# w_in's transform folded over d: two products a pair of chunks in place of four, E's coefficients through DRAM, and the third rounding step on VectorE and GpSimd

## The chip, the cores and the metric

One NeuronCore of one Trainium2 chip runs the whole kernel. The metric is device time in microseconds of one execution. The program has five engines that each run their own instructions in order and wait for one another through semaphores: TensorE (PE, with its weight loads as PEld), VectorE (DVE), ScalarE (ACT), GpSimd (POOL) and SyncE (SP), which here only issues DMAs.

## What is computed

A Fourier mixing layer and then a feed-forward layer with a squared ReLU:

```python
X = np.fft.fft(x, axis=1)                 # x: (8, 3008, 256) f32
X = np.fft.fft(X, axis=2).real            # real part only, f32
h = X.reshape(24064, 256) @ w_in          # w_in: (256, 2048)
g = np.maximum(h, 0.0) ** 2
out = g @ w_out                           # w_out: (2048, 256), out (24064, 256) f32
```

w_in and w_out arrive in double precision and are rounded to single precision inside the kernel.

## The kernel before

The second Fourier transform, over d = 256, is not done on x. Since it is linear, it is put into w_in: the kernel makes G1 (cosines over d, times w_in) and G2 (sines), each [128, 2048], and later multiplies them with Pt and Qt, the transform of x over the sequence. What is left over is column d = 128 of the frequencies, E; its part enters as a coefficient gE (one number for each of the 2048 features) times a row of E (`ew`). So one block of h is G1ᵀPt + gE·E ± G2ᵀQt.

**Pairs.** w_in and w_out come in eight pairs of 256 features each. A pair of w_in goes through four rounding steps, each a function that `convert` returns, and each a token in a written order: TS on DVE (the sign bits, L299), PW on ACT (three instructions, L306 to L308: scale the exponent, take the upper mantissa bits, and the third rounding step, a Relu into integers), H on DVE (L314, sign and exponent together), PR on GpSimd (L323, an integer addition that puts sign, exponent and mantissa together). Pairs of w_out go through the same four steps; their names have a w (TSw0 and so on). Pair 0 and 1 are rounded before the written order begins.

Then `dft_win` (L341 to L346) multiplies a rounded pair with a table over d: for cosines (`pgC`) and for sines (`pgD`) two products each, over the two halves of d, 256 columns wide. Each such product is two matmul records in the trace. `keep_win` (GC, GD; L350) copies the sums to G1 or G2 on ACT. `ends_of` (fe, L356) takes G2's last row, which holds the alternating sum, across to the partitions with two one-column products, and `keep_ends` (gE, L360) halves the result on DVE into gE.

**Order.** The string ORDER lists tokens for the first ten blocks; every token issues its instructions on its engines at that place, so the string fixes each engine's order. Besides the tokens above: f3a and f3b are the two halves of h's block 3 on TensorE (`front_half`, L986 and L988, two products of 252 columns), d3a and d3b their sums on DVE (`split_half`, L1001, L1003, L1004; the first reads gE), rl and sq the Relu and square on ACT, bk the eight records of the second layer (`plain`, L1107), sc and su the sums of w_out's parts (ACT L383, DVE L390). ph has two PSUM banks, so f waits for the d two halves earlier. H frees a raw buffer and lets SP load another pair (L285, two DMAs of 256 KB). After ORDER a regular loop runs over the blocks of eight batches, six column blocks of eight pairs each.

**Before ORDER.** The first batch of x is folded: over the sequence (`fold`: f_s, f_d; L541, L546), over d (f_sc, f_dc; L550, L554, with 129 and 128 columns left) and into even and odd frequencies (f_w, L559). f_e (L562, ACT) writes the folded column 128 into the last column of `lone`, from which the products E0 to E6 run. Each tile's products P, Q follow. Later batches are folded in pieces beside the products (`fold_later`: rows_of, columns_of, parities_of).

**Tables.** `cosd` and `sind` hold cosines and sines for d in two halves of 128, loaded by two DMAs.

Of the kernel before, what the change touches and what calls it, by code (L numbers as in the profile page):

```python
# [84 lines left out]
def kernel(  # L85
# [106 lines left out]
    cosd = const.tile([P, 2, P], F32, name="cosd")  # L192
    sind = const.tile([P, 2, P], F32, name="sind")
# [9 lines left out]
    G1 = const.tile([P, F], F32, name="G1")  # L203
    G2 = const.tile([P, F], F32, name="G2")
# [16 lines left out]
    def turn_table(t):  # L221
# [3 lines left out]
        for kp in range(2):  # L225
            nk = NC[kp][c]
            nc.scalar.mul(part_of(sinT, t)[0:rows, kp, at:at + nk], part_of(cosT, t)[0:rows, kp, at:at + nk][:, ::-1],
                          sind[0:rows, 0, P - 1:])
# [14 lines left out]
    for c in range(2):  # L243
        nc.vector.tensor_scalar(out=sind[:, c, P - 1:], in0=evens, scalar1=2.0, scalar2=-1.0,
                                op0=ALU.mult, op1=ALU.add)
# [43 lines left out]
    def convert(raw, dst, k):  # L289
# [12 lines left out]
        def powers():  # L302
# [5 lines left out]
            act(m.bitcast(U32), m, AF.Relu, bias=ramp[:, 1:2], scale=1.0)  # L308

        def halves():  # L310
            if high is None:
# [3 lines left out]
                                           op0=ALU.logical_shift_left, op1=ALU.bitwise_or)  # L315

        def product():
            to = dst()
            if high is None:
                nc.vector.tensor_copy(to, parts(low, k))  # L320
                return
            m, e = parts(st["m"], k), parts(st["e"], k)
            nc.gpsimd.tensor_tensor(out=to.bitcast(I32), in0=e.bitcast(I32), in1=m.bitcast(I32), op=ALU.add)  # L323
# [5 lines left out]
    def round_win(j, raw):  # L329
# [5 lines left out]
        return convert(raw, dst, 1)  # L335

    def round_wout(j, raw):
        return convert(raw, lambda: wout[:, j].rearrange("p h c e -> p h (c e)"), 2)

    def dft_win(j, side):  # L340

        tab, nm = ((cosd, "mC"), (sind, "mD"))[side]
        pg = psm.tile([P, CH], F32, name="pg", tag=nm) if j else psh.tile([P, CH], F32, name="pg", tag="h")
        for i in range(2):
            nc.tensor.matmul(pg, tab[:, i], win[j][:, i], start=i == 0, stop=i == 1)  # L345
        return pg  # L346

    def keep_win(j, side, pg):
        to, v = (G1, G2)[side].rearrange("p (h j f) -> j p h f", h=2, j=NJ)[j], pg.rearrange("p (h f) -> p h f", h=2)
        nc.scalar.copy(to, v)  # L350

    def ends_of(j):
        ps = psd.tile([P, CH], F32, name="pe", tag="d")
        for h in range(2):
            fc = j + NJ * h
            nc.tensor.matmul(ps[:, h:h + 1], G2[:, fc * P:(fc + 1) * P], last, start=True, stop=True)  # L356
        return ps
# [1278 lines left out]
```

## Time and profile before

| what | value |
|---|---|
| three timed runs, us | 1871.90, 1870.68, 1871.24; median 1871.24 |
| the profiled execution, its own time | 1871.07 us |
| its span, first to last instruction | 1869.3 us |
| granted TensorE clock over the span | 0.998 |
| rounding on GpSimd, L323 | 8 of w_in, 1294 ns (median); 8 of w_out, 1505 ns |
| DVE rounding steps | L299, 420 ns; L314, 684 ns, longest 1760 |
| ACT rounding steps | L306, 676 ns; L307, 756 ns; L308, 722 ns |
| products with the d tables, L345 | 64 records, 379 ns each, first at 15.5 us, last at 77.4 |
| edge products, L356 | 32 records, 250 ns each |
| copies to G1 and G2, L350 | 16, 372 ns |

A row of the timeline gives the start in us, the duration in us, engine, line, operation, what it writes and reads with its shape, how often, and in brackets how long the engine stood idle before it and who ended that. The duration of one record is not its cost on a full engine, because records overlap in the pipeline: the distance between the starts of two records that follow each other without a gap is the cost. Times below are us from the span's start.

### The profile page before, as it was taken

The page shows a single profiled execution, that of the slowest core. Times are in us where ns is not written, and L with a number is a line of the kernel's source. Part 1 is how long each engine was busy: PE and PEld are TensorE (multiplying, and loading weights), DVE is VectorE, ACT ScalarE, POOL GpSimd, SP SyncE. Part 2 cuts the span into 40 slices and gives each one's busy share as a digit, 9 for nine tenths or more (in the row PEclk, how much of TensorE's full clock was granted, in tenths as well). Part 3 has the DMA queues.
Part 4 walks back from the last instruction along what each step waited for, and adds up shares of the span by engine and source line. Part 5 has one row for each costly group of instructions (what it writes and reads, how often), then busy time and mean ns, then how long its engine had stood idle before and what let it go on. Part 6 is the DMA issues. An engine that isn't in the chain of part 4 may idle for free.

```text
span 1869.3 us, 34067 instructions
## 1 busy us (share of the span) xinstructions
PE 1854.7 (99%) x11408; PEld 1755.2 (94%) x11408; DVE 1466.6 (78%) x3480; ACT 1082.9 (58%) x1604; POOL 1465.4 (78%) x2149
## 2 busy tenths in 40 slices
PE   9999999999999999999999999999999999999998
PEld 7689999999999999999999999999999999999998
DVE  8788887887788877888788887888878887767665
ACT  5876645666466655556556565566645666444543
POOL 4489778888787887888878887788877878787886
PEclk9999999999999999999999999999999999999999
DMA  7441002100011111111011100111001100000000
GB/s 198 119 60 42 15 21 57 40 23 23 19 50 40 29 23 32 32 46 32 15 32 46 45 19 15 45 46 35 15 20 45 35 15 21 19 18 15 20 21 22
DMA packets 151309, 68.45 MB, mean 37 GB/s; under 512 B 131143, under 2 KB 142881, under 8 KB 151136
## 3 DMA queue, kind: packets, MB, share of 16 engines
q1 hardware_dynamic: 150590, 65.74, 14.0%
q8 instruction: 91, 1.49, 0.3%
q14 instruction: 82, 0.67, 0.1%
q0 software_dynamic: 416, 0.43, 0.1%
q10 hardware_dynamic: 130, 0.12, 0.0%
HBM read 41.54 MB, written 24.69 MB: 35 GB/s over the span
## 4 chain that ended last, share of the span: by engine, by line
PE 95%; DVE 3%; ACT 1%; issue 0%; POOL 0%; DMA 0%; DVEq 0%; POOLq 0%; ACTq 0%
PE F L1078 33%; PE S L1078 23%; PE hP L1015 17%; PE hQ L1015 17%; PE pd L745 2%; PE pd L868 1%; PE pd L842 1%; PE pg L345 0%; DVE wsum L390 0%; PE mA L1107 0%; PE mB L1107 0%; DVE he L1001 0%; DVE he L1019 0%; DVE g L1003 0%; PE ph L986 0%
## 5 line engine op out<-in xcount | busy, mean ns | idle before, releaser
L1028 ACT ACTIVATE g<-g 128x1008 f32<-128x1008 f32 (+1 forms) x384 | 399.4, 1040 | 304.6 <-DVE g L1024 285.3
L1019 DVE SCALAR_TENSOR_TENSOR he<-ew,gE,hP 128x252 f32<-128x252 f32 (+1 forms) x748 | 321.2, 471 | 290.2 <-PE hP L1015 290.2
L1031 ACT ACTIVATE g<-g 128x1008 f32<-128x1008 f32 (+1 forms) x384 | 399.4, 1040 | 12.1
L1015 PE MATMUL hP<-Pt,G 128*128 128x252 f32 (+1 forms) x1496 | 378.9, 376 | 3.3 <-DVE w L670 1.4
L1015 PE MATMUL hQ<-Qt,G 128*128 128x252 f32 (+3 forms) x1496 | 379.0, 376 | 0.3 <-DVE g L1024 0.3
L1078 PE MATMUL F<-s,wsum 128*128 128x168 f32 (+1 forms) x1504 | 337.1, 306 | 0.0
L1015 PEld LDWEIGHTS hQ<-Qt,G 128*128 128x128 f32 (+1 forms) x1496 | 281.9, 190 | 37.5 <-issue 2.4
L1078 PE MATMUL F<-g,wout 128*128 128x168 f32 (+1 forms) x1504 | 305.6, 305 | 0.0
L1053 POOL TENSOR_TENSOR s<-g 128x168 f32<-128x168 f32 (+1 forms) x188 | 101.3, 539 | 260.5 <-ACT g L1031 123.4
L1015 PEld LDWEIGHTS hP<-Pt,G 128*128 128x128 f32 x1496 | 265.9, 190 | 22.2 <-DVE fs L606 1.6
L1023 DVE TENSOR_TENSOR g<-he,hQ 128x504 f32<-128x504 f32 (+1 forms) x374 | 252.8, 676 | 40.1 <-DVE he L1019 2.9
L1078 PE MATMUL S<-s,wout 128*128 128x168 f32 (+1 forms) x1504 | 282.0, 306 | 0.1
L1078 PE MATMUL S<-s,wsum 128*128 128x168 f32 (+1 forms) x1504 | 275.0, 305 | 0.0
L1078 PE MATMUL F<-g,wsum 128*128 128x168 f32 (+1 forms) x1504 | 274.9, 305 | 0.0
L1024 DVE TENSOR_TENSOR g<-he,hQ 128x504 f32<-128x504 f32 (+1 forms) x374 | 250.3, 669 | 0.0
L1078 PEld LDWEIGHTS F<-s,wsum 128*128 128x128 f32 x1504 | 248.9, 190 | 0.0
L1078 PEld LDWEIGHTS F<-g,wsum 128*128 128x128 f32 x1504 | 240.6, 190 | 8.1
L1078 PEld LDWEIGHTS S<-s,wsum 128*128 128x128 f32 x1504 | 240.4, 190 | 8.2 <-issue 0.2
L1078 PEld LDWEIGHTS F<-g,wout 128*128 128x128 f32 x1504 | 240.6, 190 | 0.0
L1078 PEld LDWEIGHTS S<-s,wout 128*128 128x128 f32 x1504 | 232.2, 190 | 1.0 <-issue 0.5
L1059 POOL TENSOR_TENSOR s<-s 128x336 f32<-128x336 f32 (+1 forms) x188 | 168.6, 897 | 14.7
L1056 POOL TENSOR_TENSOR s<-s 128x336 f32<-128x336 f32 (+1 forms) x188 | 168.5, 897 | 14.7
(229 smaller groups left out, 2498.5 us busy)
## 6 DMA issues: line engine op xcount, KB each, us to landing
out_dram<-os SPq DMA_DIRECT2D x376, 56.0 KB
xt<-in_x_dram SPq DMA_DIRECT2D x39, 384.0 KB
xt<-in_x_dram SPq DMA_DIRECT2D x63, 128.0 KB
ew<-e_dram SPq DMA_DIRECT2D x39, 126.0 KB
out_dram<-os SPq DMA_DIRECT2D x288, 7.0 KB
raw<-in_moe_w_in_dram SPq DMA_DIRECT2D x16, 256.0 KB
raw<-in_moe_w_out_dram SPq DMA_DIRECT2D x16, 256.0 KB
xt<-in_x_dram SPq DMA_DIRECT2D x2, 512.0 KB
```

The costliest lines, as they stand in the source:

```text
L745: nc.tensor.matmul(ps[0:w.shape[-1]], w, part_of(cosT if lone_e else tab, t)[0:rows, kp, PLACE[t]:PLACE[t] + NC[kp][c]], start=t == ts[0] ...
L842: nc.tensor.matmul(to, left(pair[part != which]), columns(tab, TWO, o)[0:HALF2], start=True, stop=True)
L1015: nc.tensor.matmul(to[:, h, 0:n], w[:, fs], v[:, ks], start=h == 0, stop=True, skip_group_check=True)
L1019: nc.vector.scalar_tensor_tensor(out=t[:, h, 0:n], in0=window[b, k0][:, 0:n], scalar=gE[:, fc:fc + 1], in1=hP[:, h, 0:n], op0=ALU.mult, op ...
L1023: tt(out=g[:, :, 0:n], in0=t[:, :, 0:n], in1=hQ[:, :, 0:n], op=ALU.add)
L1024: tt(out=g[:, :, n:2 * n][:, :, ::-1], in0=t[:, :, 0:n], in1=hQ[:, :, 0:n], op=ALU.subtract)
L1028: act(g[:, :, 0:2 * n], g[:, :, 0:2 * n], AF.Relu)
L1031: act(g[:, :, 0:2 * n], g[:, :, 0:2 * n], AF.Square)
L1053: gt(out=s[:, 11], in0=b2[:, 0], in1=b1[:, 0], op=SUB)
L1056: gt(out=s[:, 4:6], in0=s[:, 4:6], in1=s[:, 10:11].to_broadcast([P, 2, tb]), op=SUB)
L1059: gt(out=s[:, 6:9:2], in0=s[:, 2:4], in1=s[:, 6:8], op=ADD)
L1078: nc.tensor.matmul(acc[nm][:, slot, 0:tb], w, v, start=q == 0 and nm not in begun, stop=q == NJ // 2 - 1, skip_group_check=True)
```

## The change

The products over d use that cosines and sines of even and odd frequency are symmetric or antisymmetric between d and d + 128. The two halves of w_in are added and subtracted first (`fold_win`, GpSimd), and then one table over 128 values of d is enough for the sum and one for the difference. A table's columns are 64 for cosines and 64 for sines, sorted by `sort_tables` with four ACT copies; so `dft_win` has two products, each giving half of G1 and half of G2. The partitions of G1 and G2 now hold even frequencies first and odd ones behind, and the folded x (w) is written in the same order: even columns in the first 64 places, odd ones in the next, on DVE and, in `q_beside`, on GpSimd.

```diff
+    def fold_win(j, st):
+        both = (st["e"].bitcast(F32) if "e" in st else scratch())[:, 0]
+        w = win[j]
+        gt(out=both, in0=w[:, 0], in1=w[:, 1], op=ALU.add)
+        gt(out=w[:, 0], in0=w[:, 0], in1=w[:, 1], op=ALU.subtract)
+        win[j] = both, w[:, 0]
...
+    def sort_tables():
+        q = P // 2
+        for at, (u, v) in enumerate(((cosd[:, 0::2], sind[:, 1:P - 1:2]), (sind[:, 0::2], cosd[:, 1::2]))):
+            nc.scalar.copy(TABD[at][:, 0:q], u)
+            nc.scalar.copy(TABD[at][:, q:q + v.shape[-1]], v)
...
-    def dft_win(j, side):
-        tab, nm = ((cosd, "mC"), (sind, "mD"))[side]
-        pg = psm.tile([P, CH], F32, name="pg", tag=nm) if j else psh.tile([P, CH], F32, name="pg", tag="h")
+    def dft_win(j):
+        pg = (psm.tile([P, 2, CH], F32, name="pg", tag=("mC", "mD")[j % 2]) if j else
+              psh.tile([P, 2, CH], F32, name="pg", tag="h"))
         for i in range(2):
-            nc.tensor.matmul(pg, tab[:, i], win[j][:, i], start=i == 0, stop=i == 1)
+            nc.tensor.matmul(pg[:, i], TABD[i], win[j][i], start=i == 0, stop=True, skip_group_check=True)
```

`keep_win` has two halves by partitions (GB, the upper 64, then GA, the lower), each one ACT copy of 512 elements. G2's last row, E's coefficients, goes from SBUF to DRAM and from there into gE, one value to a partition, both by SP. The edge products and the halving on DVE are gone (xe is no longer doubled either):

```diff
+    def keep_win(j, half, pg):
+        r = slice(half * P // 2, (half + 1) * P // 2)
+        to = G[r].rearrange("p a (h j f) -> j p a h f", h=2, j=NJ)[j]
+        v = pg[r].rearrange("p a (h f) -> p a h f", h=2)
+        nc.scalar.copy(to, v[:, ::-1] if half else v)
+        if half:
+            nc.sync.dma_start(out=g_dram[j:j + 1].rearrange("o (h f) -> o h f", h=2),
+                              in_=G2[P - 1:P].rearrange("o (h j f) -> j o h f", h=2, j=NJ)[j])
+    def take_ends(j):
+        nc.sync.dma_start(out=gE[:, j::NJ], in_=g_dram[j].rearrange("(h f) -> f h", h=2))
...
-            gt(out=xe, in0=xe, in1=xe, op=ADD)
```

The third rounding step stays on ACT for pairs 0 and 1 of w_in only. For the other six it is a DVE instruction behind H's, and for w_out a subtraction on GpSimd ahead of PR's addition:

```diff
-            act(m.bitcast(U32), m, AF.Relu, bias=ramp[:, 1:2], scale=1.0)
+            if k == 1 and j < 2:
+                act(m.bitcast(U32), m, AF.Relu, bias=ramp[:, 1:2], scale=1.0)
...
+            if k == 1 and j >= 2:
+                m = st["m"]
+                nc.vector.tensor_scalar(out=m.bitcast(U32), in0=m, scalar1=ramp[:, 1:2], scalar2=0.0,
+                                        op0=ALU.add, op1=ALU.max)
...
+                if k == 2:
+                    whole = st["m"].rearrange("p c e -> p (c e)").bitcast(I32)
+                    gt(out=whole, in0=whole, in1=ramp[:, 0:1].bitcast(I32).to_broadcast([P, 2 * CH]), op=ALU.subtract)
+                gt(out=to.bitcast(I32), in0=e.bitcast(I32), in1=m.bitcast(I32), op=ALU.add)
+            if k == 1:
+                fold_win(j, st)
```

The folds of x keep 128 columns in each part in place of 129 and 128. Column 128 for E is taken by f_e straight from the sums over the sequence with two or three one-column GpSimd instructions a tile, in place of one on ACT, and the copy of w's last column in `parities_of` (ACT) is gone:

```diff
-                tt(out=w[r, kp, part], in0=v[r, 0, part], in1=v[r, 1, part], op=SUB if kp else ADD)
+                tt(out=sorted_(w[r, kp, part]), in0=natural(v[r, 0, part]), in1=natural(v[r, 1, part]),
+                   op=SUB if kp else ADD)
         def f_e():
-            nc.scalar.mul(lone[r, 2 * t:2 * t + 2, P - 1:], w[r, :, H:H + 1], -1.0 if TILES[t][0] else 1.0)
+            u, v = (st["fs"][r, i, H:H + 1] for i in range(2))
+            if not TILES[t][0]:
+                for kp in range(2):
+                    gt(out=lone[r, 2 * t + kp, P - 1:], in0=u, in1=v, op=SUB if kp else ADD)
+            else:
+                gt(out=lone[r, 2 * t + 1, P - 1:], in0=v, in1=u, op=SUB)
+                gt(out=lone[r, 2 * t, P - 1:], in0=lone[r, 2 * t, P - 1:], in1=u, op=SUB)
+                gt(out=lone[r, 2 * t, P - 1:], in0=lone[r, 2 * t, P - 1:], in1=v, op=SUB)
...
-                        tt(out=w(t)[r, kp, 0:D], in0=p, in1=sc[t][r, 1, 0:D], op=SUB if kp else ADD)
-                    nc.scalar.copy(w(t)[r, :, D:], sc[t][r, :, D:])
+                        tt(out=w(t)[r, kp].rearrange("p (s o m) -> p s m o", s=2, o=2),
+                           in0=p.rearrange("p (s m o) -> p s m o", s=2, o=2),
+                           in1=sc[t][r, 1].rearrange("p (s m o) -> p s m o", s=2, o=2), op=SUB if kp else ADD)
```

Before ORDER, pair 0's products move behind P2's, `sort_tables` stands ahead of P0's, and the tables over d are loaded for 128 values of d only. In ORDER, pgC and pgD become one token pg, which stands where pgD or pgC stood, GC and GD become GB and GA, fe is gone, gE stands behind GA, and the rest keeps its order. The part around pairs 4 to 6:

```diff
-        'bk0 TSw1 H4 PWw1 PR4 TS5 Hw1 pgD4 f3a GD4 gE3 PW5 PRw1 d3b pgC4 d3a fe4 rl2 bk1 GC4 TSw2 H5 PWw2 PR5 gE4 '
-        'pgD5 TS6 Hw2 f4b GD5 sq2 f4a d4b PRw2 PW6 fe5 pgC5 d4a bk2 GC5 TSw3 H6 PWw3 PR6 TS7 rl3 pgC6 Hw3 PW7 f5b '
+        'bk0 TSw1 H4 PWw1 PR4 TS5 Hw1 pg4 f3a GB4 PW5 PRw1 d3b d3a rl2 bk1 GA4 gE4 TSw2 H5 PWw2 PR5 '
+        'pg5 TS6 Hw2 f4b GB5 sq2 f4a d4b PRw2 PW6 d4a bk2 GA5 gE5 TSw3 H6 PWw3 PR6 TS7 rl3 Hw3 PW7 f5b '
```

## The prediction

> **What bounds the kernel now.** I read the page first.
>
> ```profile
> PE 1854.7 (99%) x11408; PEld 1755.2 (94%) x11408; DVE 1466.6 (78%) x3480; ACT 1082.9 (58%) x1604; POOL 1465.4 (78%) x2149
> PE 95%; DVE 3%; ACT 1%; issue 0%; POOL 0%; DMA 0%; DVEq 0%; POOLq 0%; ACTq 0%
> ```
>
> TensorE sets the end, so a removed product is worth its time, if TensorE is also what bounds the stretch it stood in. All of w_in's transform lies before 80 us (L345 runs from 15.5 to 77.4). So next the busy times of that part, cut into four stretches (columns: length, then busy us and instructions of PE, PEld, DVE, ACT, POOL, then clock, DMA share, GB/s):
>
> ```profile
> 34.00:62.00 28.00, 27.14 (x120) 20.28 (x119) 19.73 (x50) 24.11 (x41) 9.74 (x7) 1.00 0.37 113
> 62.00:75.00 13.00, 12.86 (x46) 8.19 (x46) 8.97 (x21) 12.30 (x20) 5.60 (x4) 1.00 0.45 123
> 75.00:98.00 23.00, 23.00 (x78) 14.22 (x78) 21.75 (x59) 18.67 (x30) 9.47 (x9) 1.00 0.38 60
> ```
>
> TensorE is full, but it is not alone: ACT has 0.7 us free in the second stretch, DVE 1.25 us in the third. Only GpSimd has room. Then the timeline, where the order of the pairs is seen. Round pair 6:
>
> ```profile
> 58.85 1.03 PE L345 MATMUL pg<-win,sind 128*128 128x256 f32 x4
> 60.77 0.48 DVE L1001 SCALAR_TENSOR_TENSOR he<-ew,gE,ph 128x252 f32<-128x252 f32 x1 [2.12 <-PE ph L988]
> 62.13 0.48 DVE L1001 SCALAR_TENSOR_TENSOR he<-ew,gE,ph 128x252 f32<-128x252 f32 x1
> 63.30 0.42 DVE L299 TENSOR_SCALAR fd<-raw 128x512 uint32<-128x512 uint32 x1
> 63.63 0.69 DVE L314 SCALAR_TENSOR_TENSOR fd<-raw,fd 128x512 uint32<-128x512 uint32 x1
> 64.49 1.29 POOL L323 TENSOR_TENSOR win<-fd,m 128x512 int32<-128x512 int32 x1 [3.87 <-ACT raw L306]
> 64.57 1.76 DVE L314 SCALAR_TENSOR_TENSOR fd<-raw,fd 128x512 uint32<-128x512 uint32 x1
> 65.83 0.90 PEld L345 LDWEIGHTS pg<-win,cosd 128*128 128x128 f32 x4 [0.38 <-POOL win L323]
> ```
>
> This is a loop through four engines. The product of pair 5 (58.85) stands ahead of the block products ph; DVE's two half blocks (60.77, 62.13) wait for ph; rounding of pair 6 (63.30, 63.63) stands behind them on DVE; GpSimd ends the rounding (64.49 to 65.78); and TensorE waits 0.38 us for it. So here the loop, not TensorE's work, already sets the time. Last, the stretch before 34 us:
>
> ```profile
> 13.86 1.57 POOL L323 TENSOR_TENSOR win<-fd,m 128x512 int32<-128x512 int32 x1 [1.08 <-ACT wsum L562]
> 14.34 1.37 DVE L550 TENSOR_TENSOR sc<-fs 92x258 f32<-92x258 f32 x1
> 34.09 0.35 DVE L786 SCALAR_TENSOR_TENSOR Qt<-pd,signs,w 128x126 f32<-128x126 f32 x1 [0.17 <-PE pd L745]
> ```
>
> From 4.6 to 34.1 us DVE has no gap but that 0.17 us, and ends the stretch. L550 took 1.37 us for its usual 0.42 while GpSimd's L323 ran, and the L314 at 64.57 took 1.76 for 0.68: a DVE instruction with two inputs in SBUF stands still while GpSimd works on SBUF.
>
> **What is removed.** Two of four products a pair: each half is four matmul records, 0.86 us (58.85 to 59.71). 8 x 0.86 = 6.9 us. The edge products of L356: 55.02 to 55.39, 0.37 us, 8 x 0.37 = 3.0. TensorE is rid of 9.9 us. ACT loses 14 rounding steps L308 at 0.63 (39.42 to 40.05) = 8.8 us; DVE eight gE copies at 0.15 = 1.2.
>
> **What is added.** GpSimd: two folds of 128x256 a pair, nearest row L1251, 128x256 in 0.68, so 1.36 a pair; a subtraction of 128x512 for each of 8 wout pairs, by L323's 1.27 (below, a fold's 0.68; above, 1.51 as L323 with its strided output form). 21 us of GpSimd in all; from 34 to 98 us it is busy 24.8 of 64, so there is room, and the cost is in who waits. DVE: six tensor_scalar of 128x512 into integers: between L299's step of 0.34 (34.44 to 34.77) and L314's 0.60; I take 0.34, the same operation form. ACT: per pair two copies of 512 elements in place of two of 256; L1117 (504 elements) starts its next after 0.46, L350 after 0.27, so +0.4 a pair, 3.1 in all, less than the 8.8 removed. 20 one-column GpSimd instructions for E, at 0.20 (94x7 forms in fold_columns take 0.20) = 4.0.
>
> **Sum, by place.**
> 1) Up to 34 us: TensorE's 1.2 us for pair 0 (product 0.86, edges 0.37) gain nothing, as DVE is the full engine. Pair 0's fold (1.36) and the 15 E instructions of tiles 2 to 6 (3.0) fall among DVE instructions with two SBUF inputs. L550 lost 0.95 to an L323 of 1.57, six tenths; six tenths of the fold and four of the short ones is 2.0. Bounds: 0 (all fall in gaps) and 4.4. Moving P2's products (0.8 us) ahead of pair 0's hides most of the fold from TensorE. Table sorting on ACT hides in its 2.93 us of idleness before the first L350; without that cover, 4 x 0.28. The smaller table loads, the dropped xe+xe (0.56 on GpSimd at 146 us) and the 56 dropped ACT copies of a last column cost nothing: neither engine is late there.
> 2) Pairs 1 to 3: E's coefficients now go ACT, SP, DRAM, SP, DVE. The only such pair in the trace is e_dram's: the write issues at 100.16, the dependent read at 101.55, 1.4 us. A small DMA landed in 1.6 us (Qt to e_dram) to 3.7 (xe to e_dram); the read scatters 256 values over 128 partitions. I take 1.6, the nearer size. So 0.25 + 1.2 + 0.45 + 1.6 = 3.5 us from G's copy to gE, where L356 plus the copy took about 1. Queued behind the write's wait on SP are the raw loads (two of 0.6 us issue each), behind gE on DVE the whole half block, and behind that the PSUM bank of the next ph. Pair 2's copy ends near 42.6 (product after f1, at 41.0), behind a raw load of 1.2: gE near 47.3, where the half block began at 46.33: +1.0. Bounds: 0 and, at a landing of 3.7, +3.
> 3) Pairs 4 to 7, the loop above: +0.34 (DVE step) + 1.36 (folds) = 1.7 a pair, against 1.23 saved on TensorE that the loop does not contain (it holds one product and no edges). Pair 5: GpSimd was done at 58.10 for a product at 58.85, 0.75 of slack: +0.95. Pair 6 had none: +1.7. Pair 7 had 1.95 (71.35 to 73.30): the 1.2 of TensorE could come back, yet GpSimd now does 2.8 for wout 3 (1.27 + 1.51) between pairs 6 and 7 and bk3 waits for it; I take 0, bounds -1.2 and +1.
> 4) Blocked DVE. The two-input steps L314 lost 1.08 + 0.51 + 0.30 = 1.9 us to GpSimd between 50 and 66. GpSimd's rounding work doubles there (21 us more): +1.9. Bounds 0 and 5. From 75 to 110 the chain of waits runs through DVE (L390, L1001), so TensorE's savings there are not collected.
>
> 2.0 + 1.0 + 0.95 + 1.7 + 0 + 1.9 = +7.6. On the profiled execution's 1871.07 that is 1878.6; the median of the runs is 0.17 above that execution: **1878.8**.
>
> The Trainium skill, DMA: Bandwidth & Descriptors, Anatomy of one DMA, gives a fit with about 2.0 us fixed for each DMA of GpSimd's path, most of it the receipt of the write. This case's 1.6 for a GpSimd-issued DMA is below it, and its 3.7 above; by the page the sum would be some 0.8 higher (0.4 for each of the two DMAs), as an estimate.
>
> **Rivals.**
> A) Faster. If GpSimd's extra 1.7 a pair fits before TensorE's need, pairs 1 to 7 give 7 x 1.23 = 8.6, less 0.34 of DVE and about 2 of blocking in the full stretch from 75: -6, 1865. For it: GpSimd was idle 3 us ahead of most L323. Against: the wait at 65.83, and that it was idle because its input came late. Chance 0.17.
> B) Loop losses meet the TensorE gain of pairs 1 to 3 and 7: 1868 to 1875. Chance 0.12.
> C) E's coefficients late. If the scattered read lands as slowly as the GpSimd-issued table loads (5.9 us for 23.8 KB), each of pairs 1 to 3 waits some 3 us more, later pairs, with wider room, little: +9 on the sum's 1878.8, 1888. Against: 1 KB in place of 23.8. Chance 0.10.
> D) Scattered writes. w is now written with neighbours 64 elements apart. ACT shows such a price on reads: 94 elements at 16 B steps took 0.359 (L427), at 8 B steps 0.275 (L430), 0.9 ns an element. DVE shows none: PSUM at 16 B steps, L902, 0.264 for 94 against 0.247 (L796). If DVE pays it, L559's 26 instructions cost 26 x 0.12 = 3.0 before 34 us, and 112 of L639 cost 0.23 each, 26 us, under DVE's 20% of idle time in the batches: 1882, and up to 1900 where no idle time is near. Chance 0.10. The Trainium skill, SBUF — State Buffer, Door 1: The DMA port swizzle, bears on it: SBUF has 16-byte lines and every access that crosses to a new one pays. L427 agrees, L902 is PSUM and decides nothing.
> My forecast: 0.51.
>
> **From these the numbers.** This kernel's runs tell 0.2%, 3.7 us, from no change. Slower: my forecast, C, D: 0.71. Faster: A, 0.17. Same: 0.12. Range: down to A's edge, 1866, which leaves most of A out, and up to 1889, which holds C and D's likelier part. My forecast's own range is 1875 to 1884.
>
> **What would show it.** PE instructions 11408 - 64 = 11344. TensorE waits for GpSimd at L345's place over 5 us (now 1.6); GpSimd's busy time about 25 us up; two-input DVE steps longer than 1 us more often; the first block's last product later than now though TensorE is busy 9 us less before it. Right in step 2: a wait of DVE's L1001 place on a DMA. Wrong: if TensorE shows no new idle time before 100 us, A holds; if L559's or L639's successors take longer per element, D does; if batches after 120 us differ in length, something I have not priced.

## The result, and the profile after

The change makes the kernel slower: 1885.56 us median of 4 runs (1885.49 to 1886.64), against 1871.11 (1870.68 to 1871.90) beside it. The ratio is 1.0078, 95% interval 1.0065 to 1.0091. The profiled execution took 1885.57 us with a span of 1883.8; before it was 1871.07 and 1869.3, so 14.5 us are to be found.

From the page after, the busy times and the head of the chain:

```profile
PE 1851.0 (98%) x11344; PEld 1744.7 (93%) x11344; DVE 1492.1 (79%) x3477; ACT 1071.7 (57%) x1531; POOL 1497.1 (79%) x2190
PE 90%; DVE 3%; ACT 1%; issue 0%; POOL 0%; DVEq 0%; ACTq 0%
```

TensorE has its 64 instructions less, but holds 90% of the chain where it held 95%: work was taken away and waiting came in. GpSimd is busy 31.7 us longer, ScalarE 11.2 less. The three stretches that the prediction showed, in the same columns (length, then busy us and instructions of PE, PEld, DVE, ACT, POOL, then clock, DMA share, GB/s):

```profile
34.00:62.00 28.00, 20.82 (x74) 12.76 (x72) 25.08 (x52) 19.59 (x30) 18.46 (x18) 1.00 0.31 96
62.00:75.00 13.00, 10.13 (x33) 5.67 (x32) 9.76 (x18) 9.37 (x14) 9.46 (x9) 1.00 0.48 152
75.00:98.00 23.00, 19.29 (x57) 10.47 (x58) 19.53 (x43) 15.83 (x25) 15.47 (x14) 1.00 0.42 76
```

TensorE, full before (63.0 us of 64), works 50.2 us of 64. VectorE is now the engine nearest to full in the first stretch, and GpSimd went from 24.8 to 43.4 us. TensorE's waits after, from 30 to 110 us (engine, tile and line, what it waited for: us in total, times, longest):

```profile
PE mA L1142 <- POOL wout L332: 4.6, 4, 1.8
PE ph L1021 <- DVE g L1039: 4.5, 4, 1.8
PE pg L370 <- POOL fd L352: 2.5, 3, 1.1
PE ph L1021 <- DVE he L1036: 1.3, 1, 1.3
```

L1142 is the products with w_out of the first blocks, L370 those of the transform (L345 before), L1036 the place of L1001; L1039 ends the sums of a half block and so frees the bank for the next ph. Before, the same stretch had three waits, 1.7 us in all, of which this was the largest:

```profile
PE pg L345 <- POOL win L323: 0.9, 1, 0.9
```

The waits for GpSimd are at the fold, as forecast, and still more at w_out, whose rounding GpSimd also lengthens. Those for VectorE's half blocks, 5.8 us, are larger than either.

**Where the 14.5 us lie.** Three anchors in TensorE's timeline cut the span: the first block's broadcast product (pe), the first product of block 10 (hP), and the end. Block 10 is the first after the written-out order.

| | before | after | difference |
|---|---|---|---|
| pe of the first block | 34.49 | 36.08 | +1.6 |
| from there to block 10's first hP | 62.03 | 68.56 | +6.5 |
| from there to the end | 1772.78 | 1779.16 | +6.4 |

Within the middle part, the pairs' transforms are the marks. Pair 6 after, in the timeline:

```profile
68.77 0.48 DVE L320 TENSOR_SCALAR m<-m,ramp 128x512 uint32<-128x512 f32 x1
69.16 0.42 DVE L300 TENSOR_SCALAR fd<-raw 128x512 uint32<-128x512 uint32 x1
69.39 1.32 POOL L332 TENSOR_TENSOR win<-fd,m 128x512 int32<-128x512 int32 x1 [3.15 <-DVE m L320]
69.50 1.77 DVE L316 SCALAR_TENSOR_TENSOR fd<-raw,fd 128x512 uint32<-128x512 uint32 x1
70.79 1.06 POOL L352 TENSOR_TENSOR fd<-win 128x256 f32<-128x256 f32 x1
71.90 0.70 PE L370 MATMUL pg<-fd,tabs 128*128 128x256 f32 x2 [1.11 <-POOL fd L352]
```

It is the loop of before with two links more: VectorE's third rounding step (L320) and GpSimd's fold (L352), and TensorE waits 1.11 us for the fold. Before, its products of pair 6 did not wait:

```profile
65.27 1.01 PE L1107 MATMUL mB<-g,wout 128*128 128x504 f32 x2
66.11 1.03 PE L345 MATMUL pg<-win,cosd 128*128 128x256 f32 x4
```

The 0.38 us at 65.83 that the prediction read as TensorE's wait is that of the weight load. The products began 0.84 us after the group ahead of them, which is what that group costs (64.42 to 65.27 is 0.85). The L316 at 69.50 shows a VectorE step with two inputs held up by GpSimd: 1.77 us for its usual 0.68.

The last part is the batches, and there one group of VectorE changed: the additions that write w. After:

```profile
L674 DVE TENSOR_TENSOR w<-sp,sc 96x256 f32<-96x256 f32 x84 | 43.3, 625 | 0.5 <-ACT sp L669 0.5
L674 DVE TENSOR_TENSOR w<-sp,sc 94x256 f32<-94x256 f32 x14 | 7.7, 632 | 0.0
```

The same group before (busy us, mean ns):

```profile
L639 DVE TENSOR_TENSOR w<-sp,sc 96x256 f32<-96x256 f32 x84 | 30.1, 412 | 0.5 <-ACT sp L634 0.5
L639 DVE TENSOR_TENSOR w<-sp,sc 94x256 f32<-94x256 f32 x14 | 5.2, 411 | 0.0
```

The durations are half as long again. As records overlap, the busy times are the better price: with the remaining 14 (95 partitions, 5.2 and 7.6 us) the 112 additions keep VectorE busy 58.6 us for 40.5, 18.1 more. How that reaches TensorE is seen in one batch after:

```profile
585.06 0.67 DVE L1059 TENSOR_TENSOR g<-he,hQ 128x504 f32<-128x504 f32 x1
585.65 2.01 DVE L674 TENSOR_TENSOR w<-sp,sc 95x256 f32<-95x256 f32 x4
587.50 0.84 DVE L1054 SCALAR_TENSOR_TENSOR he<-ew,gE,hP 128x252 f32<-128x252 f32 x2
587.80 1.09 PE L1050 MATMUL hQ<-Qt,G 128*128 128x252 f32 x4 [0.40 <-DVE w L674]
```

The same place before:

```profile
574.98 1.41 DVE L639 TENSOR_TENSOR w<-sp,sc 95x256 f32<-95x256 f32 x4
576.78 0.86 DVE L1019 SCALAR_TENSOR_TENSOR he<-ew,gE,hP 128x252 f32<-128x252 f32 x2 [0.39 <-PE hP L1015]
```

Four additions take 2.01 us for 1.41, VectorE comes that much later to the half block at 587.50, and TensorE's next product stands 0.40 us. VectorE's 20% of idle time does not help, as it does not lie here: before, VectorE was idle only 0.39 us ahead of this half block. By the first hP of each batch the first batch loses 1.9 us, each of the six later ones 0.62 to 0.88, and the last none.

### The profile page after: what moved, and what is told of

Its sections match the earlier page's. It is cut to its first block, busy times and chain, and to the rows that moved or that the text cites. A ratio compares the mean times of both kernels' runs of the same rounds, so it can differ in the third digit from the quotient of the medians.

```text
span 1883.8 us, 33953 instructions
## 1 busy us (share of the span) xinstructions
PE 1851.0 (98%) x11344; PEld 1744.7 (93%) x11344; DVE 1492.1 (79%) x3477; ACT 1071.7 (57%) x1531; POOL 1497.1 (79%) x2190
## 4 chain that ended last, share of the span: by engine, by line
PE 90%; DVE 3%; ACT 1%; issue 0%; POOL 0%; DVEq 0%; ACTq 0%
PE F L1113 33%; PE S L1113 22%; PE hP L1050 16%; PE hQ L1050 16%; PE pd L903 1%; DVE w L674 1%; PE pd L877 1%; DVE he L1054 1%; PE pd L780 1%; DVE g L1058 0%; DVE g L1059 0%; DVE wsum L413 0%; ACT g L1066 0%; ACT sp L704 0%; ACT g L1063 0%
```

## The experiments

Two things made the runs hard to read. One is that the parts act through waits and do not add. The other is the clock granted to TensorE. It is 1.00 through the first 110 us before and after, but in several experiments it fell to 0.5 for 3.4 or 6.8 us. So the table below has, beside the anchors, what TensorE lost to it up to block 10: in windows of 1 us, its busy time times (1 - granted clock), summed. The last column is block 10 less that loss. It is an estimate and a lower bound, since not every lost microsecond of TensorE's is one of the span's.

| kernel | median us | ratio to before, 95% | pe | block 10 | from there on | lost to the clock | block 10 less it |
|---|---|---|---|---|---|---|---|
| before | 1871.11 | | 34.49 | 96.52 | 1772.78 | 0 | 96.5 |
| after | 1885.56 | 1.0078 [1.0065, 1.0091] | 36.08 | 104.64 | 1779.16 | 0 | 104.6 |
| e1 | 1879.81 | 1.0050 [1.003, 1.007] | 35.66 | 104.73 | 1772.97 | 0 | 104.7 |
| e2 | 1880.98 | 1.0051 [1.0028, 1.0074] | 34.67 | 101.41 | 1777.79 | 3.0 | 98.4 |
| e3 | 1887.14 | 1.0087 [1.0058, 1.0116] | 38.63 | 109.12 | 1777.98 | 6.6 | 102.6 |
| e4 | 1889.34 | 1.0099 [1.0069, 1.0128] | 37.37 | 107.58 | 1778.42 | 5.1 | 102.5 |
| e6 | 1881.43 | 1.0053 [1.0038, 1.0068] | 36.84 | 106.47 | 1772.93 | 3.3 | 103.2 |
| e7 | 1877.19 | 1.0031 [1.0019, 1.0043] | 34.96 | 97.01 | 1778.69 | 0 | 97.0 |
| e8 | 1880.75 | 1.0050 [1.0033, 1.0066] | 38.25 | 105.83 | 1773.57 | 3.4 | 102.4 |
| e9 | 1872.87 | 1.0010 [1.0001, 1.0020] | 34.54 | 97.99 | 1772.61 | 0 | 98.0 |
| e10 | 1868.63 | 0.9988 [0.9978, 0.9997] | 34.48 | 93.67 | 1772.93 | 0 | 93.7 |
| e11 | 1878.22 | 1.0032 [1.0018, 1.0045] | 39.04 | 103.88 | 1773.12 | 5.1 | 98.8 |
| e12 | 1890.98 | 1.0105 [1.0089, 1.0122] | 34.26 | 114.37 | 1774.23 | 6.2 | 108.1 |
| e13 | 1890.74 | 1.0105 [1.0090, 1.0120] | 38.46 | 114.07 | 1774.13 | 3.3 | 110.7 |

### The writes in steps: e1 and e7

e1 is the kernel after with w written in rows and the inputs read in steps of 2 instead, in all three places that make w:

```diff
-                tt(out=sorted_(w[r, kp, part]), in0=natural(v[r, 0, part]), in1=natural(v[r, 1, part]),
+                tt(out=ordered_(w[r, kp, part]), in0=parted(v[r, 0, part]), in1=parted(v[r, 1, part]),
                    op=SUB if kp else ADD)
...
-                        tt(out=w(t)[r, kp].rearrange("p (s o m) -> p s m o", s=2, o=2),
-                           in0=p.rearrange("p (s m o) -> p s m o", s=2, o=2),
-                           in1=sc[t][r, 1].rearrange("p (s m o) -> p s m o", s=2, o=2), op=SUB if kp else ADD)
+                        tt(out=w(t)[r, kp].rearrange("p (s o m) -> p s o m", s=2, o=2),
+                           in0=p.rearrange("p (s m o) -> p s o m", s=2, o=2),
+                           in1=sc[t][r, 1].rearrange("p (s m o) -> p s o m", s=2, o=2), op=SUB if kp else ADD)
```

> The sorted w is written in whole runs of 64 and its inputs are read in steps of two elements, in place of natural reads and writes that hop 64 elements each time; the values are the same. If the hop of the writes is what makes L674 take 624 ns for 412, that line returns to about 412, the seven waits of 0.4 to 0.55 us of TensorE on it go, the batches after block 10 lose 5 to 6 us, and the first stretch, where L586 has 26 instructions at 0.1 us more, 1 to 2 us: 1878 to 1880 us. If any pattern that parts even from odd columns costs the same, reading or writing, the line stays near 620 ns and the time near 1885.6.

The time from block 10 on fell from 1779.16 to 1772.97, which is that of before within 0.2 us, and block 10 did not move. The group of additions in e1:

```profile
L680 DVE TENSOR_TENSOR w<-sp,sc 96x256 f32<-96x256 f32 x84 | 30.0, 409 | 0.5 <-ACT sp L675 0.5
```

The price is back at 409 ns with the same data moved, read in steps instead of written in steps. e7 goes the other way, from the kernel before:

```diff
-                        tt(out=w(t)[r, kp, 0:D], in0=p, in1=sc[t][r, 1, 0:D], op=SUB if kp else ADD)
+                        tt(out=w(t)[r, kp, 0:D].rearrange("p (s o m) -> p s m o", s=2, o=2),
+                           in0=p.rearrange("p (s m o) -> p s m o", s=2, o=2),
+                           in1=sc[t][r, 1, 0:D].rearrange("p (s m o) -> p s m o", s=2, o=2), op=SUB if kp else ADD)
```

> The kernel before with one thing of the change alone: the 112 additions that make w in the batches write neighbouring values 64 elements apart (so the columns of the output stand in another order; nothing else differs). Theory (the later batches lose by these writes): the additions take 0.62 us for 0.41, nothing moves before 98 us, and the time is 1877 to 1878, +0.6 to +0.7 a batch and +1.9 in the first. Rival (the batches lose by something else that the stretch from 34 to 98 us hands on, such as a later start of loads): 1871 to 1872.

It came out as the theory had it: block 10 within 0.5 us of before, and 5.9 us more from there on. Its additions, from the groups:

```profile
L639 DVE TENSOR_TENSOR w<-sp,sc 96x256 f32<-96x256 f32 x84 | 42.4, 610 | 0.5 <-ACT sp L634 0.5
```

Taking the stepped writes out of the kernel after gives back 6.2 us of the last part, putting them alone into the kernel before costs 5.9. The last of the three parts is settled. (e7's additions keep VectorE busy 57.4 us, 16.9 more than before.)

### The folds: e2, e8 and e11

e2 leaves the fold out of the kernel after (the products then use the two unfolded halves, so the transform is not the reference's):

```diff
-        gt(out=both, in0=w[:, 0], in1=w[:, 1], op=ALU.add)
-        gt(out=w[:, 0], in0=w[:, 0], in1=w[:, 1], op=ALU.subtract)
-        win[j] = both, w[:, 0]
+        win[j] = w[:, 1], w[:, 0]
```

> The two fold instructions of each pair on GpSimd are left out, so the products over d take the rounded halves unfolded and G is another. If the chain DVE, GpSimd, TensorE of a pair sets the ORDER stretch, each of pairs 4 to 7 loses up to 1.5 us and the first product of block 10 comes at 100 to 101 us in place of 104.6: 1881 to 1882 us. If DVE's blocking or E's coefficients set it, block 10 moves by under 1.5 us: 1884 to 1885.

pe returned to 34.67, so pair 0's fold is 1.4 of the 1.6 us ahead of it. Block 10 came to 101.41, 3.2 us better, with TensorE's waits for w_out (3.7 us), for VectorE (3.2) and for ScalarE's copies of G (3.1) left. But the windows of e2 show a clock that the kernel after doesn't have (columns as above):

```profile
81.00:85.00 4.00, 1.31 (x5) 0.87 (x6) 3.96 (x10) 1.37 (x3) 3.28 (x4) 0.87 0.17 31
85.00:91.00 6.00, 6.00 (x8) 2.52 (x9) 5.83 (x14) 4.07 (x6) 3.25 (x3) 0.52 0.70 134
```

TensorE worked 1.31 of 4 us, and for the next 6 it was busy throughout at half its clock. With those 3.0 us set apart, the folds cost up to 6.2 in this comparison. e8 puts the folds alone into the kernel before, with all four products kept and working on the folded halves:

```diff
+            if k == 1:
+                w, both = to.rearrange("p h (c e) -> p (h c) e", c=2), st["e"].bitcast(F32)[:, 0]
+                gt(out=both, in0=w[:, 0], in1=w[:, 1], op=ALU.add)
+                gt(out=w[:, 0], in0=w[:, 0], in1=w[:, 1], op=ALU.subtract)
+                folded_in[len(folded_in)] = both, w[:, 0]
...
-            nc.tensor.matmul(pg, tab[:, i], win[j][:, i], start=i == 0, stop=i == 1)
+            nc.tensor.matmul(pg, tab[:, i], folded_in[j][i], start=i == 0, stop=i == 1)
```

> The kernel before with the two fold instructions of each w_in pair put on GpSimd between the rounding and the products, and all four products of a pair kept, working on the folded halves (so the values differ: the transform is not the reference's). Theory (the folds cost by the waits that they put into the loop, and TensorE's saved products were under cover): up to the first block product +0.8 to +1.4, pair 5 +0.6, pair 6 +1.4, time 1874 to 1876. Rival (the folds hide, and the loss between 34 and 98 us is that of the third rounding step and the DRAM route alone): time 1871 to 1872.5.

The folds did not hide, but the loss, 9.6 us in the median, is twice the most that the theory gave. Its windows around pair 0's transform show why the size was missed:

```profile
14.60:18.00 3.40, 0.93 (x6) 0.34 (x4) 3.33 (x5) 0.00 (x0) 3.18 (x3) 1.00 1.06 302
18.00:18.60 0.60, 0.60 (x3) 0.55 (x4) 0.56 (x3) 0.00 (x0) 0.00 (x0) 1.00 0.99 257
18.60:22.20 3.60, 3.60 (x13) 3.31 (x12) 3.39 (x10) 0.91 (x4) 0.00 (x0) 0.53 1.08 238
```

While TensorE waits for the fold it works 0.93 of 3.4 us, and then it gets half its clock, on average 0.53 over the next 3.6 us: 3.60 x 0.47 = 1.7 us lost, and once more from 46 us. In the kernel after, TensorE was busy 1.75 us in the same 3.4 and kept its clock. Without the loss block 10 stands at 102.4, at least 5.9 above before. e11 adds what should pay for the folds, two products a pair in place of four:

```diff
-        for i in range(2):
-            nc.tensor.matmul(pg, tab[:, i], folded_in[j][i], start=i == 0, stop=i == 1)
+        nc.tensor.matmul(pg, tab[:, 0], folded_in[j][side], start=True, stop=True)
```

> The kernel before with the two folds of each w_in pair on GpSimd and two products a pair on the folded halves (rows not put in order and the second half's table left out, so the transform is not the reference's); rounding, edge products, order of work and rows of w as before. It is the core of the change by itself. The folds alone put block 10 at 105.8 us against 96.5, and two products less should give back what they gave alone. Theory (losses by waits and gains of work do not add): 101 to 105, time 1876 to 1880. Rival (the folds cost only as TensorE is full behind them, and the shorter products take that away): 96 to 99, 1870 to 1874.

The theory's range for block 10 holds 103.9. Again half a clock is in it:

```profile
18.60:22.20 3.60, 3.60 (x14) 3.60 (x13) 3.25 (x10) 1.88 (x8) 0.00 (x0) 0.52 1.06 233
22.20:25.60 3.40, 3.40 (x9) 2.46 (x8) 3.26 (x9) 2.93 (x10) 0.00 (x0) 0.51 1.04 286
```

e11's runs also allow a check of the last column of the table. Each run with its mean granted clock:

```
1878.79 us 0.996   1878.22 us 0.996   1879.52 us 0.995   1874.32 us 0.998   1873.68 us 0.999
```

The first is the profiled one, which lost 5.1 us to the clock. The two with a mean of 0.998 and 0.999 are 4.8 us shorter than the mean of the other three. That they lacked the drops is inferred from their mean clock, as they have no profile here. If that holds, the core of the change, with the clock kept, costs some 3 us (1874.0 against 1870.8), and with the drops some 8.

### What the removed products are worth: e10

```diff
-        for i in range(2):
-            nc.tensor.matmul(pg, tab[:, i], win[j][:, i], start=i == 0, stop=i == 1)
+        nc.tensor.matmul(pg, tab[:, 0], win[j][:, side], start=True, stop=True)
```

> The kernel before with two of the four products of each w_in pair left out (one half of d only, so the transform is not the reference's); nothing is added. It prices what the change takes from TensorE: 16 products of 0.43 us, 6.9 us. Theory (the loop of rounding, product and block products sets the time from 34 to 98 us, not TensorE's work): block 10 is 0 to 3 us earlier, time 1868 to 1871. Rival (TensorE's work sets it): 5 to 6.9 us earlier, 1864 to 1866.

With nothing put in their place, 6.9 us of TensorE's work less make block 10 2.9 us earlier and the time 2.2 us shorter. pe does not move at all (34.48). This is the theory's case at its upper edge: the loop keeps the larger part of the gain. It also bounds the idea: in this order of work, the two products saved leave the folds of all eight pairs 2.2 us to spend. The edge products, 3.0 us of TensorE's work by the prediction, are still in e10, and no run prices their removal alone.

### The third rounding step: e9, e3 and e6

e9 moves it alone, in the kernel before:

```diff
-            act(m.bitcast(U32), m, AF.Relu, bias=ramp[:, 1:2], scale=1.0)
+            if k == 1 and j < 2:
+                act(m.bitcast(U32), m, AF.Relu, bias=ramp[:, 1:2], scale=1.0)
...
+            if k == 1 and j >= 2:
+                m = st["m"]
+                nc.vector.tensor_scalar(out=m.bitcast(U32), in0=m, scalar1=ramp[:, 1:2], scalar2=0.0,
+                                        op0=ALU.add, op1=ALU.max)
...
+            if k == 2:
+                whole = st["m"].rearrange("p c e -> p (c e)").bitcast(I32)
+                gt(out=whole, in0=whole, in1=ramp[:, 0:1].bitcast(I32).to_broadcast([P, 2 * CH]), op=ALU.subtract)
```

> The kernel before with the third rounding step alone moved as in the change: VectorE for w_in pairs 2 to 7, GpSimd for the w_out pairs (ScalarE keeps w_in 0 and 1); four products a pair, edge products and rows of w as before. Theory (in the kernel after without folds, TensorE still waited 3.7 us for GpSimd's w_out step and 3.2 us for VectorE, so this part costs by itself): block 10's first product 3 to 5 us later than the 96.5 of before, time 1874 to 1876. Rival (ScalarE's 8.8 us less pays for it, and what is left there is the DRAM route): within 1 us, 1870.5 to 1872.

Block 10 came 1.5 us later, between the theory's 3 to 5 and the rival's 1, and the median is 2.1 higher. ScalarE's relief buys nothing, and the price is small. e3 gives the step back to ScalarE in the kernel after (`if k == 1 and j < 2`, `if k == 1 and j >= 2` and `if k == 2` become true, false and false):

> The third rounding step is back on ACT for all sixteen pairs. It takes 0.34 to 0.48 us a pair off DVE's step ahead of GpSimd and 1.05 us of GpSimd for each pair of w_out, and puts 0.63 us on ACT, which now stands idle about 6 us in 20. If the serial chain through GpSimd sets the stretch: block 10 earlier by 1 to 3 us, 1883 to 1884.5 us. If ACT becomes the full engine again as it was at 62 to 75 us: no gain, 1885 to 1888.

Measured, that is slower by 1.6 us in the median, with TensorE waiting 4.5 us for ScalarE's copies of G. Two drops of the clock, 6.6 us, are in it. Its two runs, at mean clocks of 0.994 and 0.998, took 1888.94 and 1885.34. Whether the place of the step would tell with the clock kept, these runs leave open. e6 spreads the step over three engines, on top of e1:

```diff
+    on_dve, on_pool = {1: (2, 6), 2: (1, 3, 7)}, (4, 6)
...
-            if k == 1 and j < 2:
+            if j not in on_dve[k] and (k == 1 or j not in on_pool):
...
-            if k == 1 and j >= 2:
+            if j in on_dve[k]:
...
-                if k == 2:
+                if k == 2 and j in on_pool:
```

> The kernel after with w written in rows again (the inputs read in steps of 2) and the third rounding step of the 16 pairs divided over three engines by where each was seen idle: w_in 2 and 6 on VectorE, 3, 4, 5 and 7 on ScalarE; w_out 1, 3 and 7 on VectorE, 0, 2 and 5 on ScalarE, 4 and 6 on GpSimd. Theory 1 (the stretch from 34 us loses because GpSimd and VectorE got too much of the third step): block 10's first product, 104.7 us after the first parts, comes near 102, and the time is 1876 to 1877. Rival (the loop of rounding, fold and product loses whichever engine does the step, since the fold alone lengthens it): 104 to 106, time 1879 to 1881.

No gain over e1 (1881.43 against 1879.81), at and just above the rival's numbers, with two drops of the clock in the profiled run. With these set apart block 10 would stand at 103.2, up to 1.5 earlier than e1's, so a small gain with the clock kept is not ruled out.

### E's coefficients: e4 and e12

e4 takes them from TensorE again, in the kernel after (edge products and a copy on VectorE, no DRAM):

```diff
-    def take_ends(j):
-        nc.sync.dma_start(out=gE[:, j::NJ], in_=g_dram[j].rearrange("(h f) -> f h", h=2))
+    def ends_of(j):
+        ps = psd.tile([P, CH], F32, name="pe", tag="d")
+        for h in range(2):
+            fc = j + NJ * h
+            nc.tensor.matmul(ps[:, h:h + 1], G2[:, fc * P:(fc + 1) * P], last, start=True, stop=True)
+        return ps
+
+    def keep_ends(j, ps):
+        nc.vector.tensor_copy(gE[:, j::NJ], ps[:, 0:2])
```

> E's coefficients come by two one-column products a pair and a DVE copy as in the kernel before, not through DRAM. TensorE gets 3.0 us of work back, DVE loses its 3.3 us of waits on the coefficient's DMA. If the way through DRAM is a main loss of the ORDER stretch, block 10 comes 2 to 4 us earlier: 1882 to 1884 us. If, as the sum had it, it costs about 1 us at pair 2 alone and TensorE has idle time for the edge products: within 1 us of 1885.6.

As measured there is no gain: 3.8 us slower than after, with TensorE waiting 5.5 us for ScalarE's G at the new products and three drops of the clock (5.1 us). With the drops set apart block 10 would stand at 102.5, up to 2.1 earlier than after, which is the lower edge of the first theory. So e4 does not clear the route. e12 moves the route alone, into the kernel before:

```diff
+        if side:
+            nc.sync.dma_start(out=g_dram[j:j + 1].rearrange("o (h f) -> o h f", h=2),
+                              in_=G2[P - 1:P].rearrange("o (h j f) -> j o h f", h=2, j=NJ)[j])
...
-        nc.vector.tensor_scalar_mul(gE[:, j::NJ], ps[:, 0:2], 0.5)
+        nc.sync.dma_start(out=gE[:, j::NJ], in_=g_dram[j].rearrange("(h f) -> f h", h=2))
...
-            gt(out=xe, in0=xe, in1=xe, op=ADD)
```

> The kernel before with E's coefficients alone moved as in the change: the row of G2 goes to DRAM and comes back over the partitions, both from SyncE; the 16 edge products, the eight copies of gE with their factor 0.5 and the doubling of xe go; four products a pair, rounding and rows of w as before. Theory (step 2 of the prediction: the coefficients come 2.5 us later than by TensorE, and half blocks wait for them): block 10's first product 1 to 3 us later than 96.5, time 1871.5 to 1874. Rival (the route has cover, and TensorE's 3.0 us less count): 95 to 96.5, time 1869 to 1871.

(The first batch's E stays doubled in e12, as the fold of before makes it, so its values are not the reference's; that changes no work.) Both numbers fell far short: block 10 came at 114.4 and the time is 19.8 us longer. VectorE's largest wait of e12, from 10 to 110 us:

```profile
DVE he L1000 <- DMA gE<-g_dram: 25.4, 5, 7.0
```

One round of it, from the chain of e12 (start, length, what):

```profile
40.19 0.63 SPq L353
...
40.92 0.55 SPq L286
...
41.52 0.60 SPq L286
...
42.21 2.79 DMA gE<-g_dram
...
45.12 0.49 DVE he L1000
...
46.52 1.18 PE ph L985 x2
```

The write goes out at 40.19, two raw loads (L286) stand between it and the read, and the half block starts at 45.12, 4.9 us after the write. All the while VectorE's queue holds up, and behind the half block stands the rounding that the next raw load waits for. In the kernel after, that wait is 3.3 us in two, not 25.4 in five:

```profile
DVE he L1036 <- DMA gE<-g_dram: 3.3, 2, 3.1
```

The two transfers are the same. The rest of the change differs (one product gives both halves of G, and the written-out order puts the read elsewhere); that this is what hides the route is likely, but no run shows it. It is not hidden everywhere. Of the 3.3 us, 3.1 fall on pair 6's coefficients. SyncE's queue and VectorE there, in the kernel after:

```profile
74.06 0.63 SPq L379 DMA_DIRECT2D g_dram<-G  x1
74.79 0.81 SPq L286 DMA_DIRECT2D raw<-in_moe_w_out_dram  x2
75.70 4.20 SPq L486 DMA_DIRECT2D xe<-in_x_dram  x4
79.99 0.86 SPq L383 DMA_DIRECT2D gE<-g_dram  x1
...
82.60 0.48 DVE L1036 SCALAR_TENSOR_TENSOR he<-ew,gE,ph 128x252 f32<-128x252 f32 x1 [3.08 <-DMA gE<-g_dram]
```

The read is issued 5.9 us after the write, as SyncE issues two raw loads and four loads of xe first; for pairs 1 and 2 that distance was 1.7. From 82.60 to block 10 VectorE has no gap over 0.11 us, a w_out rounding that waits for it holds TensorE 1.83 us at 89.48, and the chain that ends at block 10 is VectorE's as far back as its view goes, to 95.16. So these 3.1 us are part of the 8.1 us, up to their whole length. How much is open, as e12 does not price the route in the kernel after.

### The folds on VectorE: e13

```diff
-        gt(out=both, in0=w[:, 0], in1=w[:, 1], op=ALU.add)
-        gt(out=w[:, 0], in0=w[:, 0], in1=w[:, 1], op=ALU.subtract)
+        tt(out=both, in0=w[:, 0], in1=w[:, 1], op=ALU.add)
+        tt(out=w[:, 0], in0=w[:, 0], in1=w[:, 1], op=ALU.subtract)
```

> The kernel after with w written in rows (inputs read in steps of 2), and the two folds of each w_in pair on VectorE in place of GpSimd. Theory (what costs is the longer chain of rounding, fold and product, by the folds' own duration: about 0.96 + 0.76 us on GpSimd, about 2 x 0.41 on VectorE): block 10's first product near 102 against 104.7 with the folds on GpSimd, time 1876 to 1878. Rival (VectorE stands waiting for GpSimd's rounding and its half blocks queue up behind): 105 or later, 1880 or more. In both, the clock granted to TensorE has to be read with it: it fell to 0.5 for 3.4 us or more after idle stretches in several of the runs, and what it took from TensorE is set apart.

The theory falls. VectorE's two largest waits from 10 to 110 us:

```profile
DVE fd L352 <- POOL win L332: 11.5, 8, 1.7
DVE he L1042 <- DMA gE<-g_dram: 4.0, 1, 4.0
```

Eight times VectorE stands still for GpSimd's rounding, and its half blocks stand behind. Here a shorter instruction on the engine that everything else queues at costs more than a long one on the engine with room.

No version here that holds the folds and computes the whole layer beats the kernel before. e1 is the whole change at its best, 1879.8.

## Why the prediction was right, and where it was not

It said 1878.8 with a range of 1866 to 1889, and slower at 0.71; the time is 1885.6. Direction and range hold. The likeliest case's own range, 1875 to 1884, does not, by 1.6 us.

**The sum, by place.** Its steps against the marks, each difference less that of the mark ahead of it. The transforms of pairs 4 to 7 begin at 52.44, 58.85, 66.11 and 73.30 us before, and at 55.25, 62.90, 71.90 and 79.28 after.

| step | forecast | measured |
|---|---|---|
| 1, up to the first block's pe | +2.0 | +1.6 |
| 2, pairs 1 to 3 (to pair 4's transform) | +1.0 | +1.2 |
| 3, pair 5 | +0.95 | +1.25 |
| 3, pair 6 | +1.7 | +1.75 |
| 3, pair 7 | 0 | +0.2 |
| 4, to block 10 | +1.9 | +2.1 |
| the sum | +7.6 | +8.1 |
| the batches | 0 in the sum, in rival D | +6.4 |

**Two steps right by luck.** Step 2 took its +1.0 from pair 2's late coefficients. In the kernel after, the half block that needs them (48.66) waits for them 0.20 us:

```profile
48.66 0.47 DVE L1036 SCALAR_TENSOR_TENSOR he<-ew,gE,ph 128x252 f32<-128x252 f32 x1 [0.20 <-DMA gE<-g_dram]
```

What holds TensorE up there is VectorE itself, which from 31.5 to 55 us has no longer gap than this one: TensorE stands 1.79, 1.28 and 1.72 us for its half blocks (at 41.13, 45.45 and 50.05), and VectorE's steps beside GpSimd's work are long (L316 1.23, 1.52 and 1.76 us, L320 0.95). That is the blocked VectorE of step 4, at the place of step 2. Step 4 forecast blocked VectorE steps behind pair 7; there pair 6's coefficients came 3.1 us late, which is the mechanism of step 2. So each mechanism was real, but stood in the other's place, and that 1.2 and 2.1 came so near to 1.0 and 1.9 is luck. Step 1's 2.0 had 0.8 for pair 0's fold and 1.2 for E's short instructions; by e2 the fold is 1.4 of the 1.6 measured. And "here the loop, not TensorE's work, already sets the time" was read off a weight load: TensorE lost nothing at 66.11, the loop had only no slack. Pair 6's +1.7 needs no more than that, and came as 1.75.

**The mis-sized term** is the scattered writes of w. Rival D had the duration of one instruction right (0.23 us more for 256 elements; measured 0.21), and the count, but records overlap, so 112 of them keep VectorE busy 18.1 us longer and not 26; and it set them "under DVE's 20% of idle time in the batches". That step failed: a third of the 18.1, 6.2 us, came out in the time, because the additions stand just ahead of a half block that TensorE's next product waits for. The other part of D, 3.0 us before 34 us, is 0.4 by e1 (pe 36.08 to 35.66). The 20% is an average. The row that mattered was VectorE's idle time ahead of that one half block, 0.39 us in the place shown above, against 0.6 us for four additions. D was also given as a case beside the forecast, with a chance of its own, where the two can both be true, and were.

**Right sum, parts less so.** e10 shows that the removed products were worth 2.9 us at block 10, where step 3 credited them with nothing. The folds cost 5 to 6 us with the clock set apart in three comparisons (e2 against after 6.2; e8 against before 5.9; e11 against e10 5.1). The first is an upper bound (3.2 with the drops left in), the other two are lower bounds (9.3 and 10.2), so the size rests on the correction. The steps had the folds at 1.36 a pair, at three places only. Each fold pair took 0.97 + 0.79 = 1.77 us against the 1.36 taken from L1251. The third step costs 1.5 (e9). These three make 5.9 + 1.5 - 2.9 = 4.5 of the 8.1; the rest is left for E's coefficients, VectorE's steps that GpSimd holds up, and how the parts meet, and no run here splits it. The two mistakes, folds too cheap and products worth nothing, met in the sum.

**The other rivals.** A, faster: against it stands e10, as even free folds leave 2.2 us, the edge products not counted. C, late coefficients: the mechanism is real, as e12 shows with 25.4 us of waiting. In the kernel after it is 3.3, nearly all at pair 6, and less because the read lands slowly, as C had it (the half block starts 2.6 us after its issue), than because SyncE issues it late. Of the signs named, the instruction count, the longer two-input steps (L316 on average 1039 ns for 802), and the wait of the half block on a DMA came. GpSimd's wait at the transform did too, but it is 4.1 us in the whole run, not over 5, as the larger wait moved to w_out's products, which the prediction had not named.

## What to carry to other kernels

Halving an engine's work is worth what its waits leave of it: price the removal alone first, by leaving the work out, and compare that with what the replacement adds to the chain that feeds the engine (here 2.2 us against 5 to 6). When an instruction that runs in every batch gets slower, look not at its engine's average idle time but at the idle time just ahead of the next instruction that the bounding engine waits for. When a small transfer is on the chain, look at what its queue issues ahead of it (here 5.9 us for 1.7). And when a layout has to be interleaved on VectorE, try reading in steps and writing in rows; steps of 2 were free to read here.

## What the runs showed of the hardware that was not expected

**Steps cost VectorE on the write, not on the read.** A float32 addition of 256 elements a partition took 0.41 us written in rows, 0.62 with neighbours 64 elements (256 bytes) apart, and 0.41 with both inputs, one in PSUM and one in SBUF, read in steps of 2 (8 bytes). The first batch's additions of 95x128, with both inputs in SBUF, took 286, 385 and 284 ns in the same three cases. The Trainium skill, SBUF — State Buffer, Door 1: The DMA port swizzle, has every access that crosses to a new 16-byte line pay, and two accesses to a line as enough for the full rate. The writes agree with it. So do the reads at 8-byte steps, two to a line: no cost shows (409 ns against 412).

**A TensorE that waits much may pay twice.** In eight of the twelve experiments the clock granted to TensorE fell to 0.5, 17 times in all before 101 us, for 3.41 us (12 times) or 6.83 (5 times), at a price of 1.5 to 1.7 or 3.0 to 3.4 us of its work each time. Before and after have no such drop in their first 110 us. The lengths are whole windows of 3.41 us, counted from the first clock record of each trace, and these windows also tell when a drop comes. Two of e8 and two of e3 (columns as above):

```profile
15.34:18.75 3.41, 1.46 (x6) 0.98 (x7) 3.31 (x8) 0.02 (x1) 2.44 (x3) 1.00 1.06 282
18.75:22.16 3.41, 3.41 (x11) 3.14 (x10) 3.20 (x10) 0.85 (x4) 0.00 (x0) 0.50 1.08 237
...
39.96:43.37 3.41, 1.93 (x9) 1.35 (x8) 3.04 (x8) 3.33 (x6) 1.08 (x1) 1.00 0.00 0
43.37:46.78 3.41, 1.71 (x8) 1.54 (x9) 2.09 (x3) 3.35 (x6) 3.25 (x4) 1.00 0.13 20
```

In the 14 traces, without their last 40 us, all 13 full-rate windows in which TensorE was busy at most 1.53 us were followed by half the clock, 4 of the 23 with 1.60 to 1.95 us, and none of those with more. In e3 TensorE was busy only 0.21 us from 41.80 to 45.20, but this stretch lies across two windows with 1.93 and 1.71, and no drop came. The Trainium skill, TensorE: Matmul & The Clock Gate, Part 1: The HAM clock gate, has a window of about 3.4 us that runs freely, and half the rate after an idle one. The lengths agree. But most windows ahead of the drops were not idle: TensorE busy for 1.53 of 3.41 us did not keep the rate. So a wait added to a full TensorE can cost more than its own length, depending on how it falls on the windows, and two kernels that differ by a microsecond of waiting can differ by three or more in time.

**GpSimd also holds up VectorE steps with one input.** L300 reads one tensor, and its mean rose from 435 to 641 ns (L299 before); one that began at 36.72, while GpSimd folded (35.79 to 37.39), took 0.95 us against its undisturbed 0.42:

```profile
36.60 0.79 POOL L353 TENSOR_TENSOR win<-win 128x256 f32<-128x256 f32 x1
36.72 0.95 DVE L300 TENSOR_SCALAR fd<-raw 128x512 uint32<-128x512 uint32 x1
```

The prediction had named steps with two inputs alone.
